# Splitting every product of an MLP into 256 columns, and Mish straight from PSUM

## The chip, the cores and the metric

The kernel runs on one core of a Trainium2 chip. The time is the device time of one execution in microseconds; the profile is one further execution, taken with the hardware profiler. Its span runs from the first to the last instruction shown, and the execution's own time is a little longer than the span.

## The reference

The kernel computes one transformer-like block on x of 2048 rows and 512 columns. A conditioning vector c gives six vectors of 512 (shifts sa, sb, scales ca, cb, gates ga, gb). The first half filters the normalised rows with a two-dimensional FFT, the second half is an MLP with a Mish activation:

```
mod = (silu(c) @ w_mod)                    # sa, ca, ga, sb, cb, gb
h = layernorm(x) * (1 + ca) + sa
x = x + ga * irfft2(rfft2(h) * (w_r + 1j * w_i))
h = layernorm(x) * (1 + cb) + sb
u = h @ w1 + b1                            # 512 -> 1376
x = x + gb * ((u * tanh(softplus(u))) @ w2)   # 1376 -> 512
```

All inputs and the output are float32.

## The kernel before

The first third of the execution (up to about 134 us) does the spectral half with matrix products; the change doesn't touch it. The rest is the MLP, and TensorE's work there is this.

A float32 operand is split in two, a high part in the type fp32r and a low part, the rest, in the same type. A product of two operands is then three: high by high, high by low and low by high. `TERMS` lists these pairs, (0, 0), (0, 1), (1, 0). `w1h` and `w1l` are the parts of w1. A tile `h2` holds the parts of the normalised, transposed input of one batch, which is two row tiles of 128 rows: `h2[:, k, 0]` is the high and `h2[:, k, 1]` the low part, for each of four chunks k of 128 input features, 256 columns (rows of x) each. High and low lie next to each other, so `h[:, k]` is 512 columns.

There are eight batches (`NB`) and six groups (`NT`) in each; `item(g)` says which. Group t = 0 has the one last feature tile with 96 features, groups 1 to 5 have two tiles of 128 features each, 11 tiles in a batch. For each group the work passes four functions:

- `up(g)` (lines 795 to 806) forms the product with w1. For each feature tile it takes a bank of PSUM, 512 columns. Four products (L803) with `w1h` over all 512 columns put high by high into the left half and high by low into the right half. Four more (L805) with `w1l` over 256 columns add low by high into the left half.
- `front(g)` (lines 808 to 814) puts the halves together for each tile: ACT reads the right half and adds the bias (L813), DVE adds the left half (L814). The result is a buffer of 512 columns, two feature tiles beside each other.
- `back(g)` (lines 816 to 831) does Mish in place on that buffer (L820, on ACT). For groups 1 to 5 DVE then makes four sums and differences of quarters (L830), since the product with w2 is done by a scheme with 7 products of half tiles in place of 8.
- `halves(g)` casts the result to its high part on ACT (L765) and subtracts it on DVE (L766), which gives `ah` and `al`; `down(g)` multiplies with w2. For groups 1 to 5 these are 7 times 3 products of 256 columns (L856), for group 0 two times 3 products of 512 columns with 96 rows (L848). They add up in four banks of the tags B and C over a whole batch.

The last batch runs its groups in the order 1, 2, 3, 4, 5, 0; its groups 3, 4, 5 and 0 use plain products of 512 columns in `last_down` (L868 and L871), into one bank A and one bank D.

One step of the loop, `mlp(s, parts)`, issues up(s), front(s), halves(s - 1), back(s) and down(s - 2), in this order on each engine's queue. In the fifth step of a batch, `transpose_in` also issues eight transposes (L693) for the next batch, two banks of four, and `split_in` reads them. `gather`, `chain` and `residual` read the four output banks of a batch and add the result to x.

PSUM has eight banks, here four tags A, B, C and D with two buffers each. `up` takes C and D for the first two groups, and then A for a group's first tile and D for its second. `transpose_in` takes A and D (for the first batch D twice).

Of the kernel before, what the change touches and what calls it, by code (L numbers as in the profile page):

```python
# [9 lines left out]
AF = mybir.ActivationFunctionType  # L10
ALU = mybir.AluOpType

P = 128
S, D, F = 2048, 512, 1376
# [8 lines left out]
TERMS = ((0, 0), (0, 1), (1, 0))  # L23
# [8 lines left out]
def tile_spectral_block(ctx: ExitStack, tc: tile.TileContext, x_d, w1_d, b1_d, w2_d,  # L32
                        c_d, xt_d, wm_d, wq_d, wz_d, kr_d, km_d, kc_d, ki_d, kf_d, kv_d, kw_d, kp_d, out_d):
    nc = tc.nc
# [33 lines left out]
    def bank(tag):  # L68
        return psum.tile([P, 512], F32, name="bank", tag=tag)

    def buf(tag, dt=F32):
        return work.tile([P, 512], dt, name="buf", tag=tag)
# [9 lines left out]
    b1n = base.tile([P, NF], F32, name="b1n")  # L82
# [84 lines left out]
    st = {}  # L167
# [418 lines left out]
    with tc.manual_schedule():  # L586
# [13 lines left out]
        for p in range(pairs):  # L600
# [34 lines left out]
            if p in (3, 5):  # L635
                i = p // 2 - 1
# [9 lines left out]
    w1h = pm.tile([P, 4, NF * P], F32R, name="w1h")  # L646
    w1l = pm.tile([P, 4, NF * P], F32R, name="w1l")
    pm.tile([P, 16], F32, name="line")
    w2 = {}
# [24 lines left out]
    def h2_tiles(b):  # L674
        if b % 2 == 0:
            h2[b] = pm.tile([P, 4, 2, 256], F32R, name="h2e", tag="h2e")
        else:
            h2[b] = big.tile([P, 4, 2, 256], F32R, name="h2o", tag="cr")
# [7 lines left out]
    def transpose_in(n, g):  # L686
        if g == 0:
            h2_tiles(n // 2)
        st["pt2", g] = ps = bank("AD"[g] if n else "D")
        hs = st["h2", n]  # L690
        for k in range(2):
            for i, h in enumerate(hs):
                nc.tensor.transpose(ps[:, (2 * k + i) * P:(2 * k + i + 1) * P],  # L693
                                    h[:, (2 * g + k) * P:(2 * g + k + 1) * P], ident)
# [48 lines left out]
    def item(g):  # L743
        b, i = divmod(g, NT)
        return b, (i + 1) % NT if b == NB - 1 else i

    def tiles(t):
        return [(0, NF - 1, F - (NF - 1) * P)] if t == 0 else [(e, 2 * t - 2 + e, P) for e in range(2)]
# [43 lines left out]
    ups, acts, out_ps, done = {}, {}, {}, {}  # L792
    tsum = modr[:, 0:2].rearrange("p r (e d) -> p (r e) d", d=256)

    def up(g):
        b, t = item(g)
        h = h2[b]
        ups[g] = []
        for e, f, rows in tiles(t):
            ps = bank("CD"[e] if g < 2 else "AD"[e])[:rows]  # L800
            fs = slice(f * P, f * P + rows)
            for k in range(4):
                nc.tensor.matmul(ps, w1h[:, k, fs], h[:, k], start=(k == 0), stop=False)  # L803
            for k in range(4):
                nc.tensor.matmul(ps[:, 0:256], w1l[:, k, fs], h[:, k, 0], start=False, stop=(k == 3))  # L805
            ups[g].append((e, f, ps))

    def front(g):
        st["w", g] = w = buf("g1")
        for e, f, ps in ups.pop(g):  # L810
            rows = ps.shape[0]
            o = w[:rows, 256 * e:256 * e + 256]
            nc.scalar.activation(o, ps[:, 256:], AF.Identity, bias=b1n[:rows, f:f + 1])  # L813
            nc.vector.tensor_tensor(o, o, ps[:, 0:256], op=ALU.add)  # L814

    def back(g):
        b, t = item(g)
        w = st.pop(("w", g))
        o = w if t else w[:96, 0:256]
        nc.scalar.activation(o, o, AF.Mish)  # L820
        if t == 0:
            return [(o, slice(0, 2))]
        if b == NB - 1 and t > 2:
            return [(w, slice(0, 4))]
        u = buf("g2")
        a = w.rearrange("p (e s) -> p e s", s=P)
        v = u.rearrange("p (e s) -> p e s", s=P)
        for o, p, q, op in ((v[:, 0], a[:, 0], a[:, 2], ALU.add), (v[:, 1], v[:, 0], a[:, 1], ALU.subtract),
                            (v[:, 2], a[:, 1], a[:, 0], ALU.subtract), (v[:, 3], a[:, 3], v[:, 1], ALU.subtract)):
            nc.vector.tensor_tensor(o, p, q, op=op)  # L830
        return [(w[:, P:], slice(0, 3)), (u, slice(3, 7))]
# [6 lines left out]
    def down(g):  # L838
        b, t = item(g)
        if b == NB - 1 and t not in (1, 2):  # L840
            return last_down(g, t)
        a = acts.pop(g)
        out = out_ps.setdefault(b, None) or [bank(n) for n in "CBBC"]
        out_ps[b] = out
        if t == 0:
            for n, half in ((1, 1), (2, 0)):
                for i, (p, q) in enumerate(TERMS):
                    nc.tensor.matmul(out[n], a[p][:96, half], w2[0][q][:96], start=(i == 0), stop=False)  # L848
            return
        last = b == NB - 1  # L850
        end = t == (2 if last else 5)
        for n, half, e, r in END if last and end else RAW + SUM:
            o = out[n][:, 256 * half:256 * half + 256]
            own = last or n in (0, 3)
            for i, (p, q) in enumerate(TERMS):
                nc.tensor.matmul(o, a[p][:, e], w2[t][q][:, r], start=(own and half == 0 and t == 1 and i == 0),  # L856
                                 stop=(end and i == 2 and (n, half) != (1, 0)), skip_group_check=own)

    def last_down(g, t):
        a = acts.pop(g)  # L860
        if t == 3:
            out_ps["last"] = bank("A"), bank("D")
        for half in range(2):
            o = out_ps["last"][half]
            for f in range(2 if t else 1):
                for i, (p, q) in enumerate(TERMS):
                    if t:
                        nc.tensor.matmul(o, a[p][:, half + 2 * f], w2["plain", t][q][:, 512 * f:512 * f + 512],  # L868
                                         start=(t == 3 and f == 0 and i == 0), stop=False)
                    else:  # L870
                        nc.tensor.matmul(o, a[p][:96, half], w2[0][q][:96], start=False, stop=(i == 2))  # L871

    rows = modr[:, 0:2]

# [34 lines left out]
    def mlp(s, parts):  # L909
        b, i = divmod(s, NT)  # L910
        nxt = 2 * b + 2 if b < NB - 1 else None
        up(s)
        if i == 4 and nxt:
            for g in range(2):
                transpose_in(nxt, g)
        front(s)
        halves(s - 1, parts)
        parts = back(s)
        if i == 3 and nxt:
            norm_pair(nxt)  # L920
        if i == 4 and nxt:
            for g in range(2):
                split_in(nxt, g)
        down(s - LAG)
        if i == 1 and b:
            gather(b - 1)
            chain(b - 1)
        if i == 2 and b:
            residual(b - 1)
        if s == total - 3:  # L930
            gather(b)
            chain(b)
        if s == total - 2:
            residual(b)
        return parts

    def finish(parts):
        b = NB - 1
        halves(total - 1, parts)
        down(total - 2)  # L940
        down(total - 1)
        for i in range(2):
            n = 2 * b + i
            nc.vector.tensor_tensor(x[:, n, :], x[:, n, :], out_ps["last"][i], op=ALU.add)
            nc.sync.dma_start(ov[:, n:n + 1, :], x[:, n:n + 1, :])
# [25 lines left out]
    for s in range(N2 + 1):  # L971
        if s < N2:
            p3_col(s)
        if s >= 1:
            p3_row(s - 1)
        if s in (7, 8):
            transpose_in(0, s - 7)
        if s == 15:
            up(0)
        if s == 16:  # L980
            up(1)
        if s >= 1:
            norm_sums(s - 1)
        for fn, *args in prep.get(s, ()):
            fn(*args)
    split_w2(0, False)
    norm_scale(N2 - 4, N2)
    front(0)
    front(1)
    h, l = (w.rearrange("p e d -> p (e d)")[:, 768:] for w in w2[3])  # L990
    nc.vector.tensor_tensor(l, tsum.rearrange("p e d -> p (e d)"), plain(h), op=ALU.subtract)
    halves(0, back(0))
    parts = back(1)
    load_w2(4)
    sum_w2(4, 0, 1, 2, 3)
# [164 lines left out]
```

## Time and profile before

| what | us |
|---|---|
| median of three runs | 379.59 |
| lowest and highest of them | 379.28, 380.18 |
| the profiled execution | 379.18 |
| its span | 377.4 |

How to read the profile: the engines are PE (TensorE's products), PEld (its loads of the stationary operand), DVE, ACT, POOL and SP. A piece of the chain of waits is its start and its length in us, the engine, the tile written, the line and how many instructions it holds. A group of instructions has the line, the engine, the operation, output and inputs with their shapes and its count, then its busy time in us and the mean of one in ns, then the time that the engine stood idle just before them and what ended it. Products are pipelined: the mean duration of one is longer than the distance from one to the next, so the pace is read from starts.

### The profile page before, as it was taken

How to read it: one execution, taken by the hardware profiler on the slowest of the kernel's cores; microseconds unless marked ns; L12 is line 12 of the kernel's file. 1: busy time of each engine (PE TensorE's matmuls, PEld its weight loads, DVE VectorE, ACT ScalarE, POOL GpSimd, SP SyncE). 2: the span in 40 equal slices, each digit the busy share in tenths (PEclk: the TensorE clock that was granted, in tenths of full speed). 3: DMA queues.
4: the chain of work that ended last, by engine and by line, in shares of the span. 5: the costliest groups of instructions: out<-in, count | busy, mean ns of one | idle time of the engine just before them, and what ended most of it. 6: DMA issues, size and time to landing. Idle time of an engine off the chain costs nothing.

```text
span 377.4 us, 7443 instructions
## 1 busy us (share of the span) xinstructions
PE 371.6 (98%) x2809; PEld 332.9 (88%) x2809; DVE 292.3 (77%) x673; ACT 240.0 (64%) x535; POOL 91.4 (24%) x110
## 2 busy tenths in 40 slices
PE   8999999999999999999999999999999999999995
PEld 8899866668999988998999999998998999999984
DVE  1898989892878979879749758857966975988993
ACT  1688856855668447964945845855765674675650
POOL 0587725861974303300000000000000100026000
PEclk9999999999999999999999999999999999999999
DMA  7999998464332211000100100100100200221011
GB/s 241 376 337 344 326 378 320 141 197 131 104 103 73 81 30 56 2 0 8 50 2 1 57 0 2 56 2 1 58 2 0 76 2 0 85 75 67 3 56 56
DMA packets 20164, 36.78 MB, mean 97 GB/s; under 512 B 3713, under 2 KB 6625, under 8 KB 19873
## 3 DMA queue, kind: packets, MB, share of 16 engines
q1 hardware_dynamic: 20128, 36.31, 28.1%
q8 instruction: 22, 0.36, 0.4%
q14 instruction: 14, 0.11, 0.1%
HBM read 32.10 MB, written 4.20 MB: 96 GB/s over the span
## 4 chain that ended last, share of the span: by engine, by line
PE 94%; DVE 2%; ACT 2%; issue 1%; ACTq 0%
PE bank L856 24%; PE bank L803 21%; PE bank L805 10%; PE bank L531 4%; PE bank L504 4%; PE bank L724 4%; PE bank L715 4%; PE bank L714 4%; PE bank L211 3%; PE bank L256 3%; PE bank L848 3%; PE bank L868 2%; PE bank L693 2%; PE bank L267 1%; PE bank L479 1%; PE bank L257 1%
## 5 line engine op out<-in xcount | busy, mean ns | idle before, releaser
L813 ACT ACTIVATE buf<-bank,b1n 128x256 f32<-128x256 f32 (+1 forms) x88 | 40.8, 472 | 62.7 <-PE bank L805 59.9
L814 DVE TENSOR_TENSOR buf<-buf,bank 128x256 f32<-128x256 f32 (+1 forms) x88 | 35.3, 416 | 35.1 <-ACT buf L813 34.4
L766 DVE TENSOR_TENSOR al<-buf,ah 128x512 fp32r<-128x512 f32 (+2 forms) x85 | 53.7, 656 | 0.7 <-ACT ah L765 0.7
L803 PE MATMUL bank<-h2e,w1h 128*128 128x512 f32 (+1 forms) x176 | 47.9, 394 | 0.0
L803 PE MATMUL bank<-h2o,w1h 128*128 128x512 f32 (+1 forms) x176 | 47.8, 393 | 0.0
L785 POOL TENSOR_TENSOR buf<-buf,modr 128x512 f32<-128x512 f32 (+1 forms) x3 | 3.9, 1299 | 179.2 <-DVE buf L814 172.1
L765 ACT CAST ah<-buf 128x512 fp32r<-128x512 f32 (+2 forms) x85 | 43.0, 548 | 1.2 <-DVE buf L830 1.1
L830 DVE TENSOR_TENSOR buf<-buf 128x128 f32<-128x128 f32 x148 | 39.8, 310 | 3.5 <-ACT buf L820 2.2
L820 ACT ACTIVATE buf<-buf 128x512 f32<-128x512 f32 (+1 forms) x48 | 28.6, 597 | 15.9 <-DVE buf L814 15.8
L856 PE MATMUL bank<-w2a,ah 128*128 128x256 f32 x161 | 34.4, 283 | 0.0
L803 PEld LDWEIGHTS bank<-h2o,w1h 128*128 128x128 f32 (+1 forms) x176 | 29.8, 185 | 4.7 <-DVE buf L814 0.4
L803 PEld LDWEIGHTS bank<-h2e,w1h 128*128 128x128 f32 (+1 forms) x176 | 29.9, 186 | 4.3
L856 PE MATMUL bank<-w2b,ah 128*128 128x256 f32 x147 | 30.6, 277 | 0.0
L805 PEld LDWEIGHTS bank<-h2e,w1l 128*128 128x128 f32 (+1 forms) x176 | 26.5, 185 | 3.9
L805 PEld LDWEIGHTS bank<-h2o,w1l 128*128 128x128 f32 (+1 forms) x176 | 26.5, 185 | 3.9
L805 PE MATMUL bank<-h2e,w1l 128*128 128x256 f32 (+1 forms) x176 | 27.5, 278 | 0.0
L805 PE MATMUL bank<-h2o,w1l 128*128 128x256 f32 (+1 forms) x176 | 27.5, 278 | 0.0
L856 PEld LDWEIGHTS bank<-w2a,ah 128*128 128x128 f32 x161 | 26.3, 188 | 0.0
L715 PE MATMUL bank<-kc,d 128*128 128x128 f32 x128 | 24.8, 275 | 0.0
L714 PE MATMUL bank<-kc,d 128*128 128x128 f32 x128 | 24.7, 275 | 0.0
L856 PEld LDWEIGHTS bank<-w2b,ah 128*128 128x128 f32 x147 | 24.0, 188 | 0.0
L127 DVE BATCH_NORM_STATS2 st<-x 128x6 f32<-128x512 f32 x32 | 22.1, 689 | 0.6
(232 smaller groups left out, 944.8 us busy)
## 6 DMA issues: line engine op xcount, KB each, us to landing
buf<-in_B_w_dram SPq DMA_DIRECT2D x20, 256.0 KB, 2.6
x<-in_A_x_dram SPq DMA_DIRECT2D x16, 256.0 KB, 4.9
xring<-in_x_t_dram SPq DMA_DIRECT2D x16, 256.0 KB, 4.8
out_dram<-x SPq DMA_DIRECT2D x7, 512.0 KB, 2.6
mraw<-in_km_dram SPq DMA_DIRECT2D x16, 128.0 KB, 4.5
wqa<-in_w_q_dram SPq DMA_DIRECT2D x4, 512.0 KB, 6.0
early<-in_w_mod_dram SPq DMA_DIRECT2D x8, 256.0 KB, 6.5
wqb<-in_w_q_dram SPq DMA_DIRECT2D x4, 512.0 KB, 7.2
```

The source lines that it names most:

```text
L127: nc.vector.bn_stats(t, x[:, n, :])
L714: nc.tensor.matmul(o, dj[:, 0:128], kc[0][:, n, :], start=True, stop=False)
L715: nc.tensor.matmul(o, dj[:, 64:192], kc[1][:, n, :], start=False, stop=True)
L765: nc.scalar.copy(h, r)
L766: nc.vector.tensor_tensor(l, r, plain(h), op=ALU.subtract)
L803: nc.tensor.matmul(ps, w1h[:, k, fs], h[:, k], start=(k == 0), stop=False)
L805: nc.tensor.matmul(ps[:, 0:256], w1l[:, k, fs], h[:, k, 0], start=False, stop=(k == 3))
L813: nc.scalar.activation(o, ps[:, 256:], AF.Identity, bias=b1n[:rows, f:f + 1])
L814: nc.vector.tensor_tensor(o, o, ps[:, 0:256], op=ALU.add)
L820: nc.scalar.activation(o, o, AF.Mish)
L830: nc.vector.tensor_tensor(o, p, q, op=op)
L856: nc.tensor.matmul(o, a[p][:, e], w2[t][q][:, r], start=(own and half == 0 and t == 1 and i == 0), stop=(end and i == 2 and (n, half) != ( ...
```

## The change

Three things are done in the MLP.

`up` forms all its products with 256 columns. For each chunk k there are now three, one for each pair of `TERMS`, and all twelve of a tile add up in the same 256 columns. The two feature tiles of a group share one bank, left and right half, of the tag A (C and D for the first two groups). The products with 512 columns in `down` for group 0 and in `last_down` become pairs with 256 columns.

`front` is one activation for each tile: Mish with the bias, read from PSUM, written to the buffer. The addition on DVE is gone, and `back` no longer does Mish.

`transpose_in` takes D for both its banks, and the last output takes two D banks in place of an A and a D.

```diff
-        st["pt2", g] = ps = bank("AD"[g] if n else "D")
+        st["pt2", g] = ps = bank("D")
...
+        ps = bank("CD"[g] if g < 2 else "A")
         for e, f, rows in tiles(t):
-            ps = bank("CD"[e] if g < 2 else "AD"[e])[:rows]
+            o = ps[:rows, 256 * e:256 * e + 256]
             fs = slice(f * P, f * P + rows)
             for k in range(4):
-                nc.tensor.matmul(ps, w1h[:, k, fs], h[:, k], start=(k == 0), stop=False)
-            for k in range(4):
-                nc.tensor.matmul(ps[:, 0:256], w1l[:, k, fs], h[:, k, 0], start=False, stop=(k == 3))
-            ups[g].append((e, f, ps))
+                for i, (p, q) in enumerate(TERMS):
+                    nc.tensor.matmul(o, (w1h, w1l)[p][:, k, fs], h[:, k, q], start=(e == 0 and k == 0 and i == 0),
+                                     stop=(e == len(tiles(t)) - 1 and k == 3 and i == 2), skip_group_check=True)
+            ups[g].append((e, f, o))
 
     def front(g):
         st["w", g] = w = buf("g1")
-        for e, f, ps in ups.pop(g):
-            rows = ps.shape[0]
-            o = w[:rows, 256 * e:256 * e + 256]
-            nc.scalar.activation(o, ps[:, 256:], AF.Identity, bias=b1n[:rows, f:f + 1])
-            nc.vector.tensor_tensor(o, o, ps[:, 0:256], op=ALU.add)
+        for e, f, o in ups.pop(g):
+            rows = o.shape[0]
+            nc.scalar.activation(w[:rows, 256 * e:256 * e + 256], o, AF.Mish, bias=b1n[:rows, f:f + 1])
 
     def back(g):
         b, t = item(g)
         w = st.pop(("w", g))
-        o = w if t else w[:96, 0:256]
-        nc.scalar.activation(o, o, AF.Mish)
         if t == 0:
-            return [(o, slice(0, 2))]
+            return [(w[:96, 0:256], slice(0, 2))]
...
-                    nc.tensor.matmul(out[n], a[p][:96, half], w2[0][q][:96], start=(i == 0), stop=False)
+                    for c in range(0, D, 256):
+                        nc.tensor.matmul(out[n][:, c:c + 256], a[p][:96, half], w2[0][q][:96, c:c + 256],
+                                         start=(i == 0 and c == 0), stop=False, skip_group_check=True)
...
-                                 stop=(end and i == 2 and (n, half) != (1, 0)), skip_group_check=own)
+                                 stop=(end and i == 2 and (n, half) != (1, 0)), skip_group_check=True)
...
-            out_ps["last"] = bank("A"), bank("D")
+            out_ps["last"] = bank("D"), bank("D")
...
-                    if t:
-                        nc.tensor.matmul(o, a[p][:, half + 2 * f], w2["plain", t][q][:, 512 * f:512 * f + 512],
-                                         start=(t == 3 and f == 0 and i == 0), stop=False)
-                    else:
-                        nc.tensor.matmul(o, a[p][:96, half], w2[0][q][:96], start=False, stop=(i == 2))
+                    for c in range(0, D, 256):
+                        if t:
+                            l, r = a[p][:, half + 2 * f], w2["plain", t][q][:, 512 * f + c:512 * f + c + 256]
+                        else:
+                            l, r = a[p][:96, half], w2[0][q][:96, c:c + 256]
+                        nc.tensor.matmul(o[:, c:c + 256], l, r, start=(t == 3 and f == 0 and i == 0 and c == 0),
+                                         stop=(t == 0 and i == 2 and c > 0), skip_group_check=True)
```

## The prediction

> **What bounds the kernel now.** I read the first part of the page, then the busy times by stage, then the chain of waits in its order of time, and last the groups of instructions and the waits.
>
> ```profile
> span 377.4 us, 7443 instructions
> PE 371.6 (98%) x2809; PEld 332.9 (88%) x2809; DVE 292.3 (77%) x673; ACT 240.0 (64%) x535; POOL 91.4 (24%) x110
> ...
> PE 94%; DVE 2%; ACT 2%; issue 1%; ACTq 0%
> ```
>
> TensorE carries 94% of the chain that ends last. The MLP is where the change lies, so I ask the same of its long middle stretch; the columns are the stretch, its length, the busy time of PE, PEld, DVE, ACT and POOL with counts, the granted clock, the DMA share and GB/s:
>
> ```profile
> 146.30:330.50 184.20, 184.20 (x1289) 170.41 (x1288) 139.52 (x333) 119.69 (x244) 4.87 (x5) 1.00 0.06 23
> ```
>
> There TensorE is busy all the time at full clock, DVE for 76% of it and ACT for 65%. So work taken from DVE or ACT there is worth nothing by itself. What counts is the rate at which products leave TensorE, and a busy time can't tell that. The chain can: with TensorE on it without a break, the pieces' starts give the pace. One batch of two row tiles, from one set of transposes (L693) to the next:
>
> ```profile
> 181.41 0.87 PE bank L693 x8
> 182.29 2.48 PE bank L856 x21
> 184.76 0.92 PE bank L803 x4
> 185.68 0.47 PE bank L805 x4
> 186.15 0.93 PE bank L803 x4
> 187.07 0.47 PE bank L805 x4
> 187.54 2.48 PE bank L856 x21
> 190.02 0.92 PE bank L803 x4
> 190.94 0.47 PE bank L805 x4
> 191.41 2.38 PE bank L856 x21
> 193.79 0.91 PE bank L803 x4
> 194.70 0.47 PE bank L805 x4
> 195.17 0.93 PE bank L803 x4
> 196.10 0.45 PE bank L805 x4
> 196.56 2.38 PE bank L856 x21
> 198.94 0.91 PE bank L803 x4
> ...
> 201.70 1.39 PE bank L848 x6
> ...
> 205.87 2.47 PE bank L856 x21
> ...
> 211.11 0.87 PE bank L693 x8
> ```
>
> The reader is to see two things. The batch takes 211.11 - 181.41 = 29.70 us. And 21 products of 256 columns (L856), the same program code each time, take either 2.38 us or 2.47 to 2.48: 0.1133 us each, or 0.1179. I call these the **quick and the sluggish pace**. A run of 256-column products keeps its pace: after 0.45 for the last four of a feature tile (196.10) come 21 quick ones, after 0.47 (187.07) 21 sluggish ones. The 512-column products (L803, 0.91 to 0.93 for four) are between: 0.2275 to 0.2325, where two quick ones would take 0.2267 and two sluggish ones 0.2357. The pace changes only across 512-column products and across the tile of 96 features (190.02 to 191.41: sluggish before, quick after). The granted clock is 1.00 throughout, so it isn't the clock. What sets the pace no row shows.
>
> **The change, part by part.** *Up products.* 88 feature tiles, each 4 products of 512 and 4 of 256 columns, become 12 of 256: the same columns in 352 more instructions. Two tiles now take 2.77 us (193.79 to 196.56; 2.76 from 198.94 to 201.70). Twenty-four products take 24 x 0.1133 = 2.72 quick or 24 x 0.1179 = 2.83 sluggish: -0.05 or +0.06 for a pair. *The 512-column products of the second half* (42 of L848, 36 of L868, 6 of L871) become twice as many of 256; L848's six go from 1.39 to 1.36 or 1.41. That is 436 splits in all. The 21 products of L856 keep their form, but would take the pace that the stream then has: d1 at 205.87 would go from 2.47 to 2.38 if quick, those at 191.41 and 196.56 from 2.38 to 2.48 if sluggish.
>
> So the sum hangs on which pace the stream keeps once nothing of 512 columns is left to change it. After the transposes the stream was sluggish (182.29), and they are not changed: with only 256-column products behind them I expect it sluggish until the tile of 96 features, which is 186.15's pair (184.76 to 187.54, 2.78 now, 2.83 then: +0.05, 7 times, +0.3 us). Behind the tile of 96 it was quick (191.41). Whether those 96 columns or the 512 columns in them made it quick isn't shown; since 96 columns stay there, now for 12 products, I take **quick from there to the next transposes**. For one batch: the tile of 96 -0.03 (190.02 to 191.41 is 1.39, 12 x 0.1133 = 1.36), four pairs at -0.05, L848 -0.03, the L856 run at 205.87 -0.09; together -0.35. There are six such stretches: -2.1 us. Bounds: all sluggish it is +0.03 + 4 x 0.06 + 0.02 + 2 x 0.10 = +0.49, or +2.9 us in six.
>
> The last batch has no transposes and no tile of 96 until its end, so it stays sluggish: five pairs +0.3, and L868's 36 products from 2.77/12 = 0.231 to 0.236, +0.2. The nine tiles before the first transposes start behind 128-column products with an unknown pace; -0.25 to +0.25, I take +0.1.
>
> *ACT and DVE.* The rows that go or change:
>
> ```profile
> L813 ACT ACTIVATE buf<-bank,b1n 128x256 f32<-128x256 f32 (+1 forms) x88 | 40.8, 472 | 62.7 <-PE bank L805 59.9
> L814 DVE TENSOR_TENSOR buf<-buf,bank 128x256 f32<-128x256 f32 (+1 forms) x88 | 35.3, 416 | 35.1 <-ACT buf L813 34.4
> ...
> L820 ACT ACTIVATE buf<-buf 128x512 f32<-128x512 f32 (+1 forms) x48 | 28.6, 597 | 15.9 <-DVE buf L814 15.8
> ```
>
> L814 (35.3 us of DVE) goes. L813 and L820 become 88 Mish from PSUM; no row shows one, the nearest of its form is L813 at 472 ns (41.5 us), the dearest L820's 597 (52.5 us); I take the first. ACT loses some 28 us, DVE 35, all beside a TensorE that is busy without a break, so worth nothing in the middle. *The new wait:* both halves of a tile pair lie in one bank, so the first half's Mish may have to wait for the second half's 12 products, 1.4 us. Behind it on ACT stand the casts of the group before (L765), wanted one step (some 5 us) later; ACT idles 59.9 us for these products already. Nothing. *Banks:* up takes one A bank a step in place of one A and one D, still two steps deep; the Mish of two steps before has long read it. Nothing.
>
> Where TensorE does stand still, the shorter chain counts. The waits of its loads (who waits for whom: us in total, times, longest), then the chain at the start of the MLP:
>
> ```profile
> PEld bank L848 <- DVE al L766: 0.5, 1, 0.5
> PEld bank L803 <- DVE buf L814: 0.4, 1, 0.4
> PEld bank L868 <- DVE al L766: 0.3, 1, 0.3
> ```
>
> ```profile
> 138.35 1.13 ACT buf L813 x3
> ...
> 139.50 1.28 ACT L820
> ...
> 141.24 0.41 ACT ah L765
> ...
> 141.68 0.80 DVE al L766
> ...
> 142.52 1.19 PE bank L848 x4
> ```
>
> Here the chain leaves TensorE: bias, table load (1.28), Mish, cast, low part. L848's products wait for it, 0.5 us by the first row. After: the table load at 138.35, three Mish at L813's pace (1.13) to 140.8, the cast to 141.2, the low part to 142.0. TensorE wants it 0.5 us before 142.52, at 142.0. This stall, about 0.5 us, goes; if the order turns out unlucky, nothing does. At the end:
>
> ```profile
> 362.21 2.77 PE bank L868 x12
> 364.98 1.15 PE bank L803 x4
> ...
> 366.60 5.65 PE bank L868 x24
> ...
> 372.97 1.38 DVE x L944 x2
> ```
>
> L803's four take 1.15 where they took 0.92 at 190.02: the last tile waits for a bank that L814 still reads (the second row of the waits), because the last output has taken one A and one D. With both from D, 0.23 goes. The 24 of L868 take 5.65 for twice 2.77: 0.11 is a wait for the low part (the third row), which DVE reaches sooner. What is late next there is TensorE itself, then L944 as now.
>
> **Sum:** -2.1 + 0.3 + 0.3 + 0.2 + 0.1 - 0.5 - 0.3 = -2.0 us. The span is 377.4 us and the profiled execution's whole time 379.18; 1.8 us lie around the span and stay. Against 379.18 the sum makes 377.2; that execution lies 0.4 under the median of the three runs shown, 379.59, which the result is held to: **377.6 us**. About 0.2% is what a measurement of this kernel can tell from no change.
>
> **The rivals.** *All sluggish* (slower). The 96 columns don't bring the stream to the quick pace; the transposes have set it sluggish and nothing changes it. For it: it is what every L856 run behind transposes shows, and the 512-column products that now restore the quick pace half of the time are gone. Against it: 191.41. +2.9 + 0.3 + 0.3 + 0.2 + 0.2 - 0.8 = +3.1: 382.7 us. A sluggish product in place of a quick one costs 4.6 ns, and each of the six stretches has 183 of them: it decides from some 430 sluggish ones among these 1098, where -2.0 + 430 x 0.0046 = 0.
>
> *The pace still changes within the batch*, at the products with 96 rows (L848) or elsewhere. Quick from the tile of 96 to L848 alone: -0.03 - 0.10 up to there, +0.12 behind, near 0 in a stretch, and +0.1 in all with the other terms: 379.7. Sluggish up to L848 and quick behind it: +0.35 - 0.19, times six, +0.9, with the rest +1.0: 380.6. For it: L848's products follow a quick tile and precede another one, with 512 columns, and nothing shows what 256 would do.
>
> *A constant price for each product*, whatever the pace: from the rows it lies between 2 x 0.1133 - 0.2325 = -0.006 us and 2 x 0.1179 - 0.2275 = +0.008, the middle +0.001, for 436 splits +0.5, with the shorter stalls -0.3: 379.3. For it: the two paces come out about even on 512-column products. Against it: two quick products are shorter than the shortest 512-column row, two sluggish ones longer than the longest, so it is no constant. The Trainium skill, page "TensorE: Matmul & The Clock Gate", section "Back-to-back issue gap", has such a constant, and it speaks against the change: isolated products cost their columns and 2.5 ns each, an estimate of +1.1 us for the 436, or 379.9 by it.
>
> *All quick.* The transposes leave the stream sluggish only because it was sluggish before them (187.07 was too). Then 7 stretches gain a further 0.3 each and the last batch 1.2: 374.3 us. Against it: TensorE restarts behind the transposes.
>
> *The change doesn't reach what bounds*: it takes work from ACT and DVE, which wait. That is so in every case above but for 0.8 us at the two ends; alone they would give 378.8.
>
> **How the numbers follow.** Quick from the tile of 96 on: 0.36. All sluggish: 0.30. The pace changes within the batch: 0.21, of it 0.15 within 0.2% of no change and 0.06 above. A constant price: 0.05, within it. All quick: 0.08. Faster 0.44, same 0.20, slower 0.36. The range goes from 375.5 to 382.9: it leaves out the all-quick case and something at each end. The likeliest case alone has 376.9 to 378.4, from the nine tiles and the two stalls.
>
> **What would show it.** In the changed kernel's chain of waits the runs of 21 products that stand at L856 now at 2.38 behind the tile of 96 features and at 2.48 behind the transposes, and pairs of tiles at 2.72 or 2.83. All at 2.48 and 2.83 is the all-sluggish rival. Products with another pace than these two make the whole sum wrong, and so does a TensorE that waits for the Mish. The start shows right if no wait stands ahead of the first products that L848 is now, the end if the last tile of 96 doesn't wait for its bank.

## The result, and the profile after

The changed kernel takes 377.47 us, the median of 16 runs (376.86 to 379.35); the kernel before takes 379.74 in the same comparison. The ratio is 0.9944, with a 95% interval of 0.9933 to 0.9955. One run of the kernel before took 1301.82 us, and its median passes over it. The profiled execution takes 377.67 us, its span 375.7.

First the page of the changed kernel: the span, the busy times by engine, and the group of the new activation.

```profile
span 375.7 us, 8202 instructions
...
PE 368.9 (98%) x3245; PEld 350.3 (93%) x3245; DVE 261.3 (70%) x585; ACT 213.2 (57%) x487; POOL 91.7 (24%) x110
...
L813 ACT ACTIVATE buf<-bank,b1n 128x256 f32<-128x256 f32 (+1 forms) x88 | 37.3, 471 | 99.5 <-PE bank L805 85.5
```

DVE and ACT have lost 31 and 27 us of work, and the span is 1.7 us shorter. What ACT no longer does stands in the last column as idle time: 99.5 us ahead of L813 where it was 62.7, and 85.5 of them end with TensorE's products. The middle stretch shows it for all engines (the columns are those of the same view before):

```profile
146.30:330.50 184.20, 184.20 (x1610) 184.20 (x1610) 114.16 (x263) 99.54 (x208) 5.02 (x5) 1.00 0.07 24
```

TensorE is busy for the whole stretch as before, with 1610 products in place of 1289, at the same clock; DVE has gone from 76 to 62% of it. So what was gained there was gained in the rate of products. The chain of waits of the changed kernel, one batch from transposes (L693) to transposes; L805 are the up products, L855 the runs of 21:

```profile
181.22 0.87 PE bank L693 x8
182.10 2.47 PE bank L855 x21
184.57 2.83 PE bank L805 x24
...
189.88 1.37 PE bank L805 x12
191.24 2.38 PE bank L855 x21
193.62 2.72 PE bank L805 x24
...
210.64 0.87 PE bank L693 x8
```

There are two paces: 2.47 to 2.48 and 2.83 (0.118 us for a product) from the transposes to the tile of 96 features at 189.88, 2.38 and 2.72 to 2.73 (0.1133 to 0.1138) from there to the next transposes. The batch takes 210.64 - 181.22 = 29.42 us, where it took 29.70.

The start and the end of the MLP in the same view:

```profile
134.35 1.37 PE bank L805 x12
...
136.61 5.66 PE bank L805 x48
142.26 1.42 PE bank L846 x12
...
151.81 0.87 PE bank L693 x8
...
328.29 0.87 PE bank L693 x8
...
363.79 1.37 PE bank L805 x12
365.16 6.14 PE bank L871 x54
```

At the start the chain doesn't leave TensorE any more: the products with 96 rows (L846) follow the up products with no ACT or DVE between. At the end the last tile of 96 takes 1.37 for its twelve, with no wait for a bank, and 54 products behind it take 6.14, which is 0.1137 each: quick.

### The profile page after: what moved, and what is told of

It is laid out like the page before. It is cut to its first block, busy times and chain, and to the rows that moved or that the text cites. A ratio compares the mean times of both kernels' runs of the same rounds, so it can differ in the third digit from the quotient of the medians.

```text
span 375.7 us, 8202 instructions
## 1 busy us (share of the span) xinstructions
PE 368.9 (98%) x3245; PEld 350.3 (93%) x3245; DVE 261.3 (70%) x585; ACT 213.2 (57%) x487; POOL 91.7 (24%) x110
## 4 chain that ended last, share of the span: by engine, by line
PE 87%; DMA 10%; DVE 1%; SPq 1%; issue 0%; DVEq 0%
PE bank L805 32%; PE bank L855 24%; PE bank L531 4%; PE bank L504 4%; PE bank L714 4%; PE bank L724 4%; PE bank L715 4%; DMA mraw<-in_km_dram 3%; PE bank L846 3%; DMA x<-in_A_x_dram 2%; DMA modr<-scb 2%; PE bank L871 2%; PE bank L693 2%; DMA xring<-in_x_t_dram 2%; PE bank L479 1%; DMA wmc<-in_w_mod_dram 1%
## 5 line engine op out<-in xcount | busy, mean ns | idle before, releaser
L766 DVE TENSOR_TENSOR al<-buf,ah 128x512 fp32r<-128x512 f32 (+2 forms) x85 | 51.9, 632 | 71.0 <-ACT ah L765 70.9
L813 ACT ACTIVATE buf<-bank,b1n 128x256 f32<-128x256 f32 (+1 forms) x88 | 37.3, 471 | 99.5 <-PE bank L805 85.5
L805 PE MATMUL bank<-h2e,w1h 128*128 128x256 f32 (+1 forms) x352 | 62.0, 278 | 0.0
L805 PE MATMUL bank<-h2o,w1h 128*128 128x256 f32 (+1 forms) x352 | 61.9, 277 | 0.0
L805 PEld LDWEIGHTS bank<-h2e,w1h 128*128 128x128 f32 (+1 forms) x352 | 52.9, 185 | 0.0
L805 PEld LDWEIGHTS bank<-h2o,w1h 128*128 128x128 f32 (+1 forms) x352 | 52.9, 185 | 0.0
L805 PE MATMUL bank<-h2e,w1l 128*128 128x256 f32 (+1 forms) x176 | 48.8, 277 | 0.0
L805 PE MATMUL bank<-h2o,w1l 128*128 128x256 f32 (+1 forms) x176 | 48.8, 277 | 0.0
L827 DVE TENSOR_TENSOR buf<-buf 128x128 f32<-128x128 f32 x148 | 42.6, 329 | 1.3
L855 PE MATMUL bank<-w2a,ah 128*128 128x256 f32 x161 | 34.5, 283 | 0.0
L805 PEld LDWEIGHTS bank<-h2e,w1l 128*128 128x128 f32 (+1 forms) x176 | 32.6, 185 | 0.0
L805 PEld LDWEIGHTS bank<-h2o,w1l 128*128 128x128 f32 (+1 forms) x176 | 32.6, 185 | 0.0
L855 PE MATMUL bank<-w2b,ah 128*128 128x256 f32 x147 | 30.6, 277 | 0.0
L855 PEld LDWEIGHTS bank<-w2a,ah 128*128 128x128 f32 x161 | 26.3, 188 | 0.0
L855 PEld LDWEIGHTS bank<-w2b,ah 128*128 128x128 f32 x147 | 24.0, 188 | 0.0
L256 PE MATMUL bank<-buf,mring 128*128 128x512 f32 x48 | 20.9, 435 | 0.9 <-DVE buf L249 0.9
L714 PEld LDWEIGHTS bank<-kc,d 128*128 128x128 f32 x128 | 19.5, 192 | 0.5 <-ACT d L394 0.3
```

What stands on the lines that cost most here:

```text
L256: nc.tensor.matmul(pa, m[:, a, 0:128], g, start=(i == 0), stop=False)
L714: nc.tensor.matmul(o, dj[:, 0:128], kc[0][:, n, :], start=True, stop=False)
L766: nc.vector.tensor_tensor(l, r, plain(h), op=ALU.subtract)
L805: nc.tensor.matmul(o, (w1h, w1l)[p][:, k, fs], h[:, k, q], start=(e == 0 and k == 0 and i == 0), stop=(e == len(tiles(t)) - 1 and k == 3 a ...
L813: nc.scalar.activation(w[:rows, 256 * e:256 * e + 256], o, AF.Mish, bias=b1n[:rows, f:f + 1])
```

## The experiments

**Theory** after the result: the pace is a state that the stream of products carries along. Products with 96 columns of weights bring it to the quick pace; transposes and short waits leave it sluggish; products of 256 columns with 128 columns of weights change nothing. **Rivals**: the tile's place in the loop, or something else near it, does it; or the gain comes from the shorter ACT and DVE work.

All runs are compared with the kernel before. The median of 0.9944 x 379.6 = 377.5 us is the mark for "as the changed kernel". The last column is the MLP alone, in the one profile of each run: the span less the start of the first piece of up products (375.7 - 134.35 = 241.35 for the changed kernel; 377.4 - 133.91 = 243.49 before). It leaves out the first third, which no edit touches.

| run, all edits made to the changed kernel | median us | ratio to before, 95% | MLP in the profile, us |
|---|---|---|---|
| the changed kernel | 377.47 | 0.9944 (0.9933 to 0.9955) | 241.35 |
| e1: tile of 96 formed with 128 columns, shifted by 32 | 380.68 | 1.0012 (0.9994 to 1.0030) | 244.10 |
| e9: the same with an aligned slice | 383.79 | 1.0074 (1.0045 to 1.0103) | 246.57 |
| e5: 96 columns in nine products right behind the transposes | 376.34 | 0.9914 (0.9895 to 0.9934) | 239.58 |
| e10: the same in three products | 375.77 | 0.9882 (0.9858 to 0.9905) | 239.74 |
| e2: 512 columns again in L846 | 380.24 | 0.9998 (0.9984 to 1.0012) | 243.46 |
| e6: transposes one run of 21 later | 377.51 | 0.9949 (0.9931 to 0.9968) | 240.97 |
| e7: tile of 96 first in the last batch | 376.94 | 0.9931 (0.9917 to 0.9945) | 240.44 |
| e8: e6 and e7 together | 376.59 | 0.9926 (0.9909 to 0.9943) | 239.91 |
| e3: transposes ahead of the tile of 96, short preparation | 384.80 | 1.0119 (1.0097 to 1.0140) | 248.18 |
| e4: bias and Mish apart again | 378.43 | 0.9955 (0.9938 to 0.9973) | 242.43 |
| e11: e3 with an earlier preparation | 375.81 | 0.9897 (0.9880 to 0.9914) | 239.54 |
| e12: e11 and e7 together | 377.05 | 0.9911 (0.9885 to 0.9936) | 240.20 |

### Is it the 96 columns?

**e1.** All twelve products of the last feature tile read 128 columns of w1, the 32 ahead of the tile and its own 96.

```diff
-            fs = slice(f * P, f * P + rows)
+            fs = slice(f * P + rows - P, f * P + rows)
...
-                    nc.tensor.matmul(o, (w1h, w1l)[p][:, k, fs], h[:, k, q], start=(e == 0 and k == 0 and i == 0),
+                    nc.tensor.matmul(full, (w1h, w1l)[p][:, k, fs], h[:, k, q], start=(e == 0 and k == 0 and i == 0),
```

> The last feature tile of each batch is formed with 128 columns of w1 in place of 96 (columns 1248 to 1375, of which the first 96 results are used, so the output is not the reference's). Theory: the 96 columns are what brings the stream of products to the quick pace (0.1133 us), and transposes bring it to the sluggish one (0.1179). Without the 96 columns all six stretches of 183 products stay sluggish, 6 x 183 x 4.6 ns = +5.0 us, and the last products of all +0.3: about 382.8 us, with every run of 21 products at 2.48. Rival: it is the place of that tile, or that it is a step with one tile alone, not its columns: no change, 377.5.

It came between: 380.68. The chain of this kernel (its lines are one further down: L806, L856 for L805, L855) shows the run behind the tile in two batches:

```profile
162.23 2.47 PE bank L856 x21
...
192.40 2.38 PE bank L856 x21
```

Of the six stretches three stay sluggish, as the first shown, and three turn quick, as the second, one by one in turn: those whose batch is read from the input tile h2e turn. So neither theory held as written: 128 columns lose the effect half of the time, but a slice shifted by 32 columns can have it too.

**e9** takes the shift away: the last tile reads columns 1152 to 1279, aligned like every other tile; the rest is as in e1.

```diff
-            fs = slice(f * P, f * P + rows)
+            fs = slice(f * P, f * P + P) if t else slice(9 * P, 10 * P)
```

> The last feature tile is formed with 128 columns of w1 again, now with the tenth tile's columns 1152 to 1279 in its place, which lie in the same grid of 128 as all other tiles (the output is not the reference's). In the run with columns 1248 to 1375 three of the six stretches turned quick all the same. Theory: it was the shift by 32 columns that disturbed the stream there, and 128 columns in the grid keep the pace: all six stretches sluggish, +5.0 and +0.3 at the end, 382.8 us, runs of 21 at 2.48 throughout. Rival: the place of that tile has a part of its own: some stretches turn quick, 377.5 to 380.5.

As the theory said: 383.79. In the chain every piece is sluggish, from transposes to transposes:

```profile
185.45 0.87 PE bank L693 x8
...
194.10 1.41 PE bank L806 x12
195.52 2.47 PE bank L856 x21
...
215.66 0.87 PE bank L693 x8
```

The batch takes 215.66 - 185.45 = 30.21 us. The tile stands at the same place with the same number of products and columns of input; only the weights' slice differs, and with its columns the rows written, 128 in place of 96. The place does nothing by itself. The MLP takes 246.57 us, 5.2 more than the changed kernel's; 5.0 and 0.3 were named.

**e5** puts products with 96 columns at another place: the ninth feature tile, the first in the step behind the transposes, has 96 columns in nine of its twelve products.

```diff
+                some = 96 if f == 8 and k else rows
+                fs = slice(f * P, f * P + some)
...
```

**e10** has them in three of the twelve, all else equal (shown against e5).

```diff
-                some = 96 if f == 8 and k else rows
+                some = 96 if f == 8 and k == 1 else rows
```

> Of the ninth feature tile of each batch, the first of the step behind the transposes, nine of the twelve products use 96 columns of w1 in place of 128 (32 features miss three quarters of their sum, so the output is not the reference's). Theory: products of fewer columns in a stream that runs at the sluggish pace bring it to the quick one wherever they stand, except right behind transposes. Then some 43 products in each of seven stretches and 228 in the last batch become quick: (7 x 43 + 228) x 4.6 ns = -2.4, 375.1 us, and the run of 21 behind that step at 2.38. Rival: it is the place of the last tile, the first that reads the next batch's h2, and not its columns: 377.5, with that run at 2.48.

> As the run with nine products of 96 columns in the ninth feature tile, but with three of them (32 features miss a quarter of their sum, so the output is not the reference's). Theory: in the changed kernel the third product of the last tile is quick already, so three are enough: 375.2 us, with the run of 21 behind that step at 2.38. Rival: the quick pace is only kept up by products of fewer columns, and the full ones behind three of them fall back: 377.5.

e5 came to 376.34, short of the 375.1 named but clear of the rival; e10 to 375.77. The chain of e10, the run behind the ninth tile in the first batch and then the second batch from behind the transposes on:

```profile
157.75 2.47 PE bank L856 x21
...
181.88 2.48 PE bank L856 x21
184.35 2.74 PE bank L806 x24
187.10 2.38 PE bank L856 x21
```

The pair at 184.35 turns within itself (2.74), and the run at 187.10, which was 2.48, is 2.38. Three products with 96 columns are enough there and in six more batches, away from the tile of 96. In the first batch they aren't: the run at 157.75 is sluggish, and it is the tile of 96 that turns the stream; nine products turn it in all eight batches of e5. In e5 the batch takes 29.22 us, 0.20 less than the changed kernel's; e10's takes 29.22, the same, so the difference between their medians isn't put down to the edit. Both fall short of the sum in the last batch: a run of 21 takes 2.56 there, and the sluggish pace follows until the ninth tile; e11 below looks at this.

### What else changes the pace?

**e2** makes L846's twelve products six of 512 columns again.

```diff
-                    for c in range(0, D, 256):
-                        nc.tensor.matmul(out[n][:, c:c + 256], a[p][:96, half], w2[0][q][:96, c:c + 256],
-                                         start=(i == 0 and c == 0), stop=False, skip_group_check=True)
+                    nc.tensor.matmul(out[n], a[p][:96, half], w2[0][q][:96],
+                                     start=(i == 0), stop=False, skip_group_check=True)
```

> Line 846's twelve products of 256 columns are six of 512 again, nothing else. Theory: a product of 512 columns can change the pace, one of 256 can't. In the kernel before, six such products were followed by a run at the sluggish pace, with two feature tiles of 512-column products between; here the 69 products from there to the transposes would be sluggish, 6 x 69 x 4.6 ns = +1.9, and the six themselves 1.39 in place of 1.37: 379.5 us. Rival: the 512-column products keep the pace that they find: +0.1, 377.6.

380.24: the ratio, 0.9998, is that of the theory. The chain of e2 (here L845 for L846):

```profile
199.74 2.72 PE bank L805 x24
202.46 1.39 PE bank L845 x6
203.85 2.83 PE bank L805 x24
```

Six products of 512 columns stand between a quick pair and a sluggish one. With them the whole gain is gone (0.9998): splitting the products of the up tiles gained nothing measurable while these six stayed.

**e6** issues the transposes behind the step's 21 products, so that one run less stands between them and the tile of 96. **e7** lets the last batch take its groups in the order 0 to 5, so that its tile of 96 comes first. **e8** does both.

```diff
         up(s)
-        if i == 4 and nxt:
-            for g in range(2):
-                transpose_in(nxt, g)
...
+        down(s - LAG)
         if i == 4 and nxt:
             for g in range(2):
+                transpose_in(nxt, g)
+            for g in range(2):
                 split_in(nxt, g)
-        down(s - LAG)
```

```diff
         b, i = divmod(g, NT)
-        return b, (i + 1) % NT if b == NB - 1 else i
+        return b, i
...
```

> The transposes stand behind the 21 products of their step in place of ahead of them. Theory: the sluggish stretch begins at the transposes, so it gets shorter by these 21 products, seven times: 7 x 21 x 4.6 ns = -0.7, 376.8 us, with that run at 2.38. Rival: what is sluggish are the products that read w2a, wherever the transposes stand, or ACT, which now waits 2.4 us longer for the transposes, holds up the products: 377.5 or more.

> The last batch runs its groups in the order of the others, so the tile with 96 features is its first and not its last; the plain products start with it. Theory: the last batch then runs quick from its first tile on, 228 products x 4.6 ns = -1.05: 376.4 us. Rival: that tile changes the pace only with what stands behind it in the other batches, or the end gets longer because the last products now wait for a longer chain: 377.5 or more.

> The transposes behind the 21 products of their step, and the last batch in the order of the others, together. Theory: both gains, -0.7 and -1.05: 375.8 us. Rival: as for the two alone, 377.5 or more.

The medians, 377.51, 376.94 and 376.59, lie 0.5 to 0.8 us above what the theory named, and the intervals of e6 and e7 overlap with the changed kernel's, so the medians don't decide. The chains do. First e6, then e7's last batch:

```profile
182.07 2.38 PE bank L855 x21
184.45 0.87 PE bank L693 x8
185.32 2.83 PE bank L805 x24
```

```profile
338.32 1.37 PE bank L805 x12
...
364.18 8.17 PE bank L871 x72
```

The run that was moved ahead of the transposes is quick in e6, and what follows the transposes is sluggish. In e7 the last batch turns quick at 338.32 and stays so to the end (8.17/72 = 0.1135). The batch of e6 takes 29.32 us (184.45 to 213.77), 0.10 less than the changed kernel's. By the MLP's time the three gain 0.4, 0.9 and 1.4 us, where 0.7, 1.05 and 1.75 were named: the right way, and less.

### Transposes directly ahead of the tile of 96

**e3.** From the second batch on the transposes stand ahead of the tile of 96, so that nothing sluggish is left between. The rows that they read are normalised one step before, behind that step's casts on ACT.

```diff
+        at = 4 if b == 0 else 0
+        if i == 0 and nxt:
+            for g in range(2):
+                transpose_in(nxt, g)
         up(s)
...
-        if i == 3 and nxt:
+        if i == 3 and b == 0:
             norm_pair(nxt)
-        if i == 4 and nxt:
+        if i == 5 and b < NB - 2:
+            norm_pair(nxt + 2)
...
```

> From the second batch on, the transposes for the next batch stand ahead of the tile with 96 features, not in the fifth step; the normalisation for them a step before. Theory: the sluggish pace that transposes leave lasts no product now, and six stretches of 66 products and 228 in the last batch become quick, 624 x 4.6 ns = -2.9: 374.6 us, runs of 21 at 2.38 everywhere from the second batch on. Rival 1: what is sluggish there belongs to the tiles w2a and w2hi that those products read, not to the transposes: 377.5, with 2.48 at the same places. Rival 2: the transposes wait for the normalisation or hold up the products in their new place: 377.5 or more, with a wait at L693.

384.80, the second rival. The chain of e3 at its boundaries, from the second on:

```profile
192.72 0.98 PE bank L693 x7
...
195.12 2.47 PE bank L855 x21
...
223.83 0.98 PE bank L693 x7
...
226.21 2.38 PE bank L855 x21
...
253.97 0.98 PE bank L693 x7
```

Ahead of each of these the chain lies on ACT for 3.25 us (from 189.47 to 192.72), which does Mish, casts and only then the normalisation (L161). TensorE doesn't stand still for all of that. Its timeline has the step's run of 21 in it, of which the last product and then the first transpose are

```profile
191.65 0.28 PE L855 MATMUL bank<-w2hi,al 128*128 128x256 f32 x1
192.02 0.33 PE L693 MATMUL bank<-ident,buf 128*128 128x128 f32 x1
```

and the next transpose starts at 192.72. At the sluggish pace and at 0.11 us for a transpose they would start at 191.77 and 192.13, so TensorE waits for about 0.25 and 0.59, 0.8 us in all. A batch that is quick throughout takes 253.97 - 223.83 = 30.14 us here, 1.0 more than in e11 below, which has no such wait. At the first boundary TensorE waits a further 0.9 us for a low part of w2 (L766). The pace behind the tile of 96 is sluggish in the first two batches with the new order (195.12 is in the second) and quick at 226.21 and in all later ones. Why the tile didn't turn the stream in those two is open.

**e11** asks for the same with the normalisation ahead of the step's Mish on ACT, and begins at the third batch.

```diff
+        at = 4 if b < 2 else 0
+        if i == at == 0 and nxt:
+            for g in range(2):
+                transpose_in(nxt, g)
         up(s)
...
+        if i == 5 and 1 <= b < NB - 2:
+            norm_pair(nxt + 2)
         front(s)
...
```

> As the run with the transposes ahead of the tile with 96 features, but the normalisation for them stands ahead of the step's Mish on ACT, not behind its casts, and the new order begins with the third batch. Theory: in that run the transposes waited some 1.9 us a batch for the normalisation, which ate the gain; the pace behind them was quick from the fourth batch on. Without the wait, five stretches of 66 products and 228 in the last batch are quick: 558 x 4.6 ns = -2.6, less some 0.05 in each tile of 96 that starts sluggish: 375.2 us, no wait at L693. Rival: right behind transposes the tile of 96 doesn't bring the quick pace in this order, as in two batches of that run: all of these batches sluggish, 5 x 183 x 4.6 ns = +4.2 in place of the gain, 381 or more.

375.81, ratio 0.9897 (0.9880 to 0.9914): it beats both kernels, and its interval lies clear below the changed kernel's. Its chain, from one batch's transposes to the next, and then in the last batch:

```profile
220.63 0.87 PE bank L693 x8
...
222.87 2.38 PE bank L855 x21
...
249.75 0.87 PE bank L693 x8
...
350.02 2.57 PE bank L855 x21
```

The batch is quick from end to end: 249.75 - 220.63 = 29.12 us between the starts of its transposes. It lacks e3's wait, which was 1.0 us a batch and not the 1.9 that the expectation took. In the last batch a run of 21 takes 2.57, 0.1 us and more beyond either pace, and the stream is sluggish behind it (2.83 for the pair at 352.59). That, too, the expectation didn't have, and the time is 0.6 above the 375.2 named.

No row of waits names what this run waits for, but the timeline narrows it. The run is the first to write the last batch's four output banks, the same that the batch before has used. Its seventh product is the first for the third of them, and L893 reads that bank for the batch before:

```profile
349.81 0.69 DVE L893 TENSOR_TENSOR modr<-bank,buf 128x512 f32<-128x512 f32 x1
350.56 0.51 PE L855 MATMUL bank<-w,ah 128*128 128x256 f32 x2
```

L893 ends at 350.50, and the seventh product begins at 350.56. In e3, e5 and e10 the same run has the same stall (2.56 to 2.57), with the same 0.06 us, and 0.05 in e5, from the end of that read to the seventh product. In the changed kernel that read ends at 350.64, the seventh product begins at 350.91, and the run takes 2.47. So the quick stream seems to catch up with a bank that DVE still reads; no run moves that read to show it.

**e12** adds e7's order to e11, to spare the last batch that loss.

> The run with the transposes first and the early normalisation, and the last batch in the order of the others, together. In the first of these a wait of about 0.12 us in the last batch (a run of 21 at 2.57) was followed by the sluggish pace for some 110 products. Theory: a wait in the stream does what transposes do. In the other order the products there don't need the banks that DVE still reads, and the tile of 96 stands first, so the last batch stays quick to its end: 110 x 4.6 ns + 0.12 = -0.6, 375.2 us, all runs of 21 at 2.38 from the third batch on. Rival: the pace turned sluggish there for another reason, such as the tiles read: no change, 375.8.

377.05 where 375.2 was named. The stall comes back at another place, in the chain of e12:

```profile
342.18 2.62 PE bank L855 x21
344.80 2.83 PE bank L805 x24
```

The timeline of DVE there has the low parts late (start, length, count of the group):

```profile
339.95 3.84 DVE L766 TENSOR_TENSOR al<-buf,ah 128x384 fp32r<-128x384 f32 x3
```

Three subtractions take 3.84 us where one has a mean of 632 ns in the changed kernel, and they end after the run of 21 has begun. The run's 2.62 is 0.24 above the quick pace of 2.38, and the stream is sluggish from there to the end. It was quick up to then, as in e11; the order costs what it was to spare.

### Is it the shorter ACT and DVE work?

**e4** gives ACT its two passes back: bias out of PSUM, then Mish in place. The addition on DVE stays away.

```diff
-            nc.scalar.activation(w[:rows, 256 * e:256 * e + 256], o, AF.Mish, bias=b1n[:rows, f:f + 1])
+            nc.scalar.activation(w[:rows, 256 * e:256 * e + 256], o, AF.Identity, bias=b1n[:rows, f:f + 1])
...
+        o = w if t else w[:96, 0:256]
+        nc.scalar.activation(o, o, AF.Mish)
...
```

> ACT's first pass over PSUM is the bias alone again, and Mish a second pass over the buffer, as before; the products stay as in the changed kernel. Theory: ACT has room beside the products, so only the chain at the start of the MLP grows, by a pass of 0.4 and less: 377.5 to 378.0. Rival: the gain came from the shorter chain of ACT and DVE: 379 or more.

378.43 (0.9955), not told apart from the changed kernel by its interval. The chain of e4 at the start and around one batch:

```profile
134.87 1.37 PE bank L805 x12
...
139.99 0.84 ACT buf L813 x2
...
153.37 0.87 PE bank L693 x8
...
182.80 0.87 PE bank L693 x8
...
212.21 0.87 PE bank L693 x8
```

The batch takes 212.21 - 182.80 = 29.41 us, as in the changed kernel, so Mish straight from PSUM does nothing there. The start does differ: the chain leaves TensorE again, and from the first up product to the first transposes it takes 153.37 - 134.87 = 18.50 us, where the changed kernel takes 151.81 - 134.35 = 17.46. So Mish from PSUM is worth about 1.0 of the changed kernel's 2.1 us (by the MLP's time 242.43 against 241.35), all of it at the start; the gain in pace stands without it.

## Why the prediction was right

The time named was 377.6 us, the result is 377.47, and for most of it the mechanism is the one that was named. At the start and at the end the sizes of terms were off, and there it is luck that they made up for each other. Step by step:

**The pace, quick from the tile of 96 to the next transposes (-2.1) and sluggish behind them (+0.3).** Right in every row. For one batch -0.35 and +0.05 were named, -0.30; it was 29.42 - 29.70 = -0.28. From the transposes at 181.22 to the last at 328.29 the changed kernel takes 147.07 us for five batches. From the first transposes to the last it was 329.88 - 151.72 = 178.16 and is 328.29 - 151.81 = 176.48: -1.7, where -2.1 and +0.3 were named. The rival of all sluggish was real: e9 is that case, with a batch of 30.21, 0.79 above the changed kernel's. The step worked out 183 products for a stretch at 4.6 ns each, 0.84. The prediction left open whether 96 columns or the 512 columns in them turn the stream. It is not the 512 columns, since the changed kernel has none; e9, e5 and e10 show the 96 columns of weights. That the 96 columns would do it was a choice, taken from the one turn at 191.41; the rival's chance (0.30), near the forecast's, was fair to what the trace of before showed.

**The other rivals of pace.** All quick is out: the stream is quick ahead of the transposes at 210.64 and sluggish behind them in every batch. The ground given against it, that TensorE restarts behind the transposes, no row of the chain shows: the run at 182.10 follows them without a wait. A change of pace at the products with 96 rows is out as well: the pairs ahead of L846 and behind it take 2.72 and 2.73. With 512 columns in those products it would have come true (e2).

**No new wait in the middle, and nothing for ACT's and DVE's time.** Right. e4 shows the same batch with the ACT pass back, and Mish from PSUM takes 471 ns, against the 472 taken from L813. ACT lost 27 us where 28 were named. DVE lost 31 where 35 were named, since its sums (L830 before, L827 now) take 42.6 us in place of 39.8, among other things; in the middle that cost nothing.

**The nine tiles at the start (+0.1) and the stall there (-0.5).** The sum of -0.4 stood against -0.35 measured: in the kernel before the first up piece stands at 133.91 and the first transposes at 151.72, so 17.81 became 17.46.

```profile
133.91 0.92 PE bank L803 x4
...
151.72 0.87 PE bank L693 x8
```

But the terms were larger than taken, on both sides. All but the first twelve products are sluggish (5.66/48 = 0.1179), and the two tiles of a bank are read only when both are done: e4's ACT chain starts 5.12 us after the first up product (139.99 - 134.87), where it was 4.44 before (138.35 - 133.91). So the two-pass form would have lost 0.7 there, and the short chain is worth 18.50 - 17.46 = 1.0, not 0.5. The new wait, which was costed at nothing, does cost at the start, and what hid it there is the shorter chain. That the sum came out at the start is luck: +0.7 and -1.0 stand in the place of +0.1 and -0.5.

**The last batch (+0.3), L868's products (+0.2), the two waits at the end (-0.3).** The five pairs are sluggish at 2.83, and the chain no longer shows the waits. The term that was mis-sized is L868's: it took the stream as sluggish to the end, and missed that the last batch's own tile of 96 (363.79) turns it as every other does. The 54 products behind it take 6.14; at the sluggish pace they would take 54 x 0.1179 = 6.37. With 1.37 in place of 1.41 for the tile, 0.27 us of +0.2 + 0.3 was not paid. From the last transposes to the end of the span it was 47.52 us before (377.4 - 329.88) and is 47.41 (375.7 - 328.29): -0.1, where the three terms make +0.2.

```profile
329.88 0.87 PE bank L693 x8
```

In all, from the first up piece to the end of the span: 243.49 (377.4 - 133.91) became 241.35 (375.7 - 134.35), -2.1 us, where -2.0 was named.

**A constant price for each product** is out: e9 and the changed kernel have the same number of products of the same length, and their MLPs differ by 5.2 us (246.57 and 241.35). The Trainium skill, page "TensorE: Matmul & The Clock Gate", section "Back-to-back issue gap", gives an isolated product its columns at 2.4 GHz and 2.5 ns, an estimate of 109.2 ns for 256 columns. The rows have 113.3 or 117.9 ns at a granted clock of 1.00, so the trace doesn't agree with it for this stream.

**Open** is what in TensorE makes the pace. Products with fewer columns of weights turned the stream but for two tiles in e3 and the first batch of e10, a shifted slice of 128 columns turned it half of the time (e1), and products of 512 columns move it down (e2) where the kernel before had them move it both ways. Fewer columns of weights always went with fewer rows written, so the runs don't tell these two apart. A disturbance of the rhythm of weight loads could fit this; no run shows it.

## What to carry to other kernels

Where TensorE is busy without a break, read the pace of equal runs of products from the starts in the chain, not from busy time: two values of the same code show a state that something in the loop sets, and a change of it is worth more than work taken from idle engines. Find what resets it (here transposes, short waits, longer products) and what restores it (here a few products with fewer columns of weights), and put the one directly ahead of the other, as e11 does for 1.7 us more (375.81 against 377.47). Prepare the moved step early enough on its own engine, or the wait costs more than the gain (e3: 1.0 us in a batch, where the quick pace gains 0.3).

## What the runs showed of the hardware

A stream of equal products kept one of two paces, 0.1133 or 0.1179 us for 256 columns, over whole batches at an unchanged clock (e9 and e11), and three products with 96 columns of weights were enough to turn it in seven batches of eight (e10). In e3, e5, e10, e11 and e12 a stall that made a quick run of 21 some 0.2 us longer (2.56 to 2.62 in place of 2.38) was enough to turn it back for all that followed, up to the next products with 96 columns. And three low-part subtractions on DVE took 3.84 us in e12, about twice their usual 3 x 0.632 = 1.9, while GpSimd worked beside them at the weights; that GpSimd was the cause wasn't tried.
